# Two of four first-chunk L tiles loaded instead of made, chunk data ahead of weights, and a later fold

## The chip, the cores and the metric

The kernel runs on one core of one Trainium2 chip. Its time is device microseconds of one execution. Three runs of the kernel before gave 573.85, 575.32 and 575.48 us, so the median is 575.32.

## The reference, cut to what matters

A chunked state-space layer is followed by two feed-forward layers. Everything is float32.

```python
# x (4, 8, 768, 32), a (4, 8, 768), B and C (4, 8, 768, 16)
for c in range(nc):                                  # along the sequence
    cum = np.cumsum(log(a_chunk), -1)
    L = np.exp(cum[..., :, None] - cum[..., None, :]) * causal
    M = np.einsum('bhin,bhjn->bhij', Cc, Bc) * L
    y[:, :, sl] = M @ xc + (Cc @ state) * exp(cum)
    state = exp(sum(la)) * state + sum_j(Bc_j xc_j * exp(cum_end - cum_j))
h = y @ w_in                                         # 3072 x 256 by 256 x 2048
g = np.where(h > 0, h, np.exp(np.minimum(h, 0)) - 1) @ w_out    # 2048 x 256
out = (((g @ w1) * (g @ w2)) @ w3) @ w_out2          # 256 x 1024, 1024 x 1024, 1024 x 256
```

## The kernel before, in words

The 3072 tokens are 6 tiles of 512, and each tile is four chunks of 128 tokens; a chunk is two sub-chunks of 64. Every large product is made of three: each operand is split into a high part (a rounding to `fp32r`, by ScalarE) and a low part (a subtraction), and `mm3` (L239) issues lo by hi, hi by lo and hi by hi.

**The chunk stage.** For chunk k, `at_load` brings one 512 KB tile `xbc` with x, B and C. The decay matrix L (a scan along the row of `a`, `at_prep`, L334) needs each row of `a` on 64 partitions. For chunks 0 to 3 TensorE spreads it: `at_wide` multiplies the split rows `cut[0]` by the selector `sel` and leaves two chunks' rows in PSUM, called for chunks 0 and 1 and, as "aw" in `ORDER`, for chunks 2 and 3. From chunk 4 on two loads per chunk spread the rows from `a_cut`, a clipped copy of `a` in HBM that the kernel writes first. Then come: `bd` on GpSimd, the products cb (C by B) and their product with L on VectorE (`decayed`, L359), the products u and the state (`states`, L396), `cd` on GpSimd, the products y (L416, L422), and `x_made`, which writes the tile's columns as xTh and xTl. The decay `pr` of a tile is made by `at_decay` (clip L261, scan L303).

**Tile 0** is ordered by hand in `ORDER`: a number is a step of the chunk stage (four per chunk: prep, cb, state, y), `"pr"` is `at_decay(0)`, and a pair (i, stage) advances the i-th weight piece: stage 2 is its bits (L146, L147, L148: the weights come as pairs of words, and two VectorE and one ScalarE operations put each float32 word together), stage 3 its parts (high and low). Piece 0 is wi0, then wi1, wi2, wo0 and so on in the order in which units need them. `"h"` is `first_half`: the products of the first unit for the first 256 of its 512 columns, which need chunks 0 and 1 only. Later tiles' chunks are placed between the units by `place`.

**The units.** `unit_a` is 256 rows of h = x w_in (12 matmuls, exp, relu, max, split), `unit_b` adds them to the second product (12 matmuls), `unit_c` is w1 and w2 and their product, `unit_d` the last product. `unit_w` makes 128 rows of w3 w_out2, the fold, once for all tiles: 24 matmuls of 256 columns each, for which two pieces of w3 (wc) and, the first time, the four pieces of w_out2 (wq) have to be ready. The fold's eight units stand between the b units of tiles 1, 2 and 3: three, four and one. Third-layer units come only when tiles 0 to 3 are through the second.

**Weights.** `weights_for` advances each piece some time (`LEADS`) ahead of its due time, which comes from the units' planned costs (`COST`) and, backwards, at least `PACE` apart. The raw words of wb (w2) lie in the rooms of the fold's wq, those of wa (w1) in the two rooms of the fold's split w3, so their loads wait for the last fold unit. The low part is made by VectorE for w_in and w_out (L722) and by GpSimd for all other weights.

**Queues.** All DMAs are issued by SyncE, in order; the order of each engine's instructions is what a timeline simulation at build time gives, under the orders laid down by `pace` and the program. The load order at the start is L706 to L719.

Of the kernel before, what the change touches and what calls it, by code (L numbers as in the profile page):

```python
# [7 lines left out]
F32 = mybir.dt.float32  # L8
F32R = mybir.dt.float32r
# [6 lines left out]
SUB = 2  # L16
R = Q // SUB
# [13 lines left out]


LEADS = ((10.0, 6.0), (16.0, 10.0), (20.0, 15.0))
PACE, LATE, END, FIRST = 1.5, 12.0, 7.0, 8.0
SPILL, BACK = 3, 8

ORDER = [0, 4, 1, "pr", 2, "aw", (0, 2), 5, 3, 6, (0, 3), 8, 7, 9, (1, 2), 10, 12, 11, 13, (1, 3), 14, "h", 15, (2, 2), (3, 2)]


XCOLS = (("x", DM), ("bn", NH * N), ("bt", 2 * R), ("cz", 2 * 2 * R), ("cp", SUB * 2 * R))  # L40
# [3 lines left out]
def kernel(  # L44
# [33 lines left out]
    eye2 = const.tile([P, SUB, R], F32, name="eye2")  # L78
    eye = const.tile([P, NH, R], F32, name="eye")
    side = const.tile([P, 2], F32, name="side")  # L80
    sel = const.tile([SUB * CPT, CPT, SUB, R], F32R, name="sel")
    begun = const.tile([P, CPT * SUB, R], F32, name="begun")

    def constants():

        V.memset(side, 0.0)
        A.activation(side, side, AF.Exp)

        G.memset(eye2, 1.0)
        G.affine_select(out=eye2, in_=eye2, compare_op=ALU.is_equal, fill=0.0, base=0,  # L90
                        pattern=[[-R, SUB], [-1, R]], channel_multiplier=1)
        n = SUB * CPT
        A.copy(sel, eye2[:n, 0, :n].rearrange("p (k s o) -> p k s o", k=CPT, o=1).to_broadcast([n, CPT, SUB, R]))
        V.tensor_tensor(out=eye2[:, 0], in0=eye2[:, 0], in1=eye2[:, 1], op=ALU.add)
        V.tensor_copy(eye, eye2[:, 0:1].to_broadcast([P, NH, R]))
        G.memset(begun, 0.0)
# [12 lines left out]
    def banks(name):  # L109

        return ps_w.tile([P, 2, TT], F32, tag="w", name=name)
# [127 lines left out]
    def mm3(out, whi, wlo, xhi, xlo, first, last, **kw):  # L239
        last_mm[:] = [T.matmul(out, wlo, xhi, start=first, stop=False, **kw).ins]  # L240
        T.matmul(out, whi, xlo, start=False, stop=False, **kw)  # L241
        T.matmul(out, whi, xhi, start=False, stop=last, **kw)  # L242
# [17 lines left out]
    def clip(eng, out, v):  # L260
        return eng.tensor_scalar(out, v, 1e-6, 1.0, op0=ALU.max, op1=ALU.min)  # L261

    def at_first():


        t = act.tile([P, 2, NH, R], F32, tag="p", name="a_f")[:SUB * NCHUNK, 0]
        nc.sync.dma_start(t, a_s)
        clip(V, t, t)
        V.memset(t[:, :, 0:1], 0.0)
        n = SUB * CPT  # L270
        hl = act.tile([P, 2, NH, R], F32R, tag="p", name="a_hl")[:n]
        split(hl[:, 0], hl[:, 1], t[:n], V)
        cut.extend([hl, t])

    def at_load(k):
        c = ck[k]
        all_ = att.tile([P, XC], F32, tag="xbc", name=f"xbc{k}", bufs=4)
        nc.sync.dma_start(all_, xc[k])
        cols_ = {}
        at = 0  # L280
        for nm, n in XCOLS:
            cols_[nm] = all_[:, at:at + n]
            at += n
        c["x"], c["bn"] = cols_["x"], cols_["bn"].rearrange("p (h n) -> p h n", h=NH)
        c["bt"] = cols_["bt"].rearrange("p (g j) -> p g j", g=2)
        c["cz"] = cols_["cz"].rearrange("p (g f) -> p g f", g=2)
        c["cp"] = cols_["cp"].rearrange("p (s f) -> p s f", s=SUB)
# [17 lines left out]

    def at_l(k):
        c = ck[k]
        c["L"] = att.tile([P, NH, R], F32, tag="L", name=f"L{k}", bufs=3)
        if k >= CPT:

            for s in range(SUB):
                nc.sync.dma_start(c["L"][R * s:R * s + R].rearrange("p h s -> p (h s)"),
                                  a_cut[SUB * k + s:SUB * k + s + 1].rearrange("s h i -> s (h i)").to_broadcast([R, NH * R]))

    def at_wide(k):


        wide = ps_a.tile([P, 2, TT], F32, tag="acc", name=f"aw{k}") if k else banks(f"aw{k}")
        for j in range(2):
            for p in range(2):  # L320
                mm = T.matmul(wide[:, j], sel[:, k + j].rearrange("r s i -> r (s i)"),
                              cut[0][:, p].rearrange("r h i -> r (h i)"), start=p == 0, stop=p == 1)
                if j == p == 0:
                    tc.keep_in_program_order(mm)
            ck[k + j]["a"] = wide[:, j]

    def at_prep(k):

        c = ck[k]
        L = c["L"]  # L330
        flat = wide = L.rearrange("p h s -> p (h s)")
        if k < CPT:
            wide = c["a"]
        made = V.tensor_tensor_scan(out=flat, data0=wide, data1=eye.rearrange("p h s -> p (h s)"), initial=0.0,  # L334
                                    op0=ALU.mult, op1=ALU.add)
        pace(made)
        if k < CPT:
            last_mm[:] = [made.ins]
        c["bd"] = att.tile([P, NH, N], F32, tag="bd", name=f"bd{k}")
        G.tensor_tensor(out=c["bd"], in0=c["bn"], in1=L[:, :, R - 1:R].to_broadcast([P, NH, N]), op=ALU.mult)  # L340
# [85 lines left out]
    def x_made(k, both, hi_eng):  # L426
        t, s0 = k // CPT, (k % CPT) * Q
        if k % CPT == 0:
            xT[t] = [act.tile([P, 2, TT], F32R, tag=f"xx{p}", name=f"xT{p}{t}", bufs=3) for p in ("h", "l")]
        hi, lo = (v[:, :, s0:s0 + Q].rearrange("p g (s i) -> p s g i", s=SUB) for v in xT[t])  # L430
        (A.copy if hi_eng is A else V.tensor_copy)(hi, both)
        return V.tensor_tensor(out=lo, in0=both, in1=hi.bitcast(F32), op=ALU.subtract)
# [11 lines left out]
    def at_chunk(k, y):  # L444


        room = banks(f"s{k}")
        cb, u, both = (room[:, :, a:b] for a, b in ((0, 4 * R), (4 * R, 4 * R + 2 * D), (4 * R + 2 * D, 6 * R + 2 * D)))
        both = by_head(both)
        last_mm[:] = [cb_products(k, cb).ins]  # L450
        u_products(k, u)
        if y is not None:
            y_products(y, both)
        decayed(k, cb)
        states(k, u)
        if y is not None:
            x_made(y, both, V)

    def ahead_of(k):

# [36 lines left out]

    gt, pt, x2, accs = {}, {}, {}, {}

    early_h = []  # L500

    def products(h, t, n, cs):
        for j in range(2):
            fs = slice((2 * n + j) * P, (2 * n + j + 1) * P)
            for k in range(2):
                mm3(h[:, j, cs], w_in_s[0][:, k, fs], w_in_s[1][:, k, fs], xT[t][0][:, k, cs], xT[t][1][:, k, cs],
                    k == 0, k == 1)

    def first_half():

        early_h.append(banks("h0_0"))
        products(early_h[0], 0, 0, slice(0, TT // 2))

    def unit_a(t, n):

        early = early_h and (t, n) == (0, 0)
        h = early_h[0] if early else banks(f"h{t}_{n}")
        products(h, t, n, slice(TT // 2 if early else 0, TT))
        e = tmp(f"e{t}_{n}")
        A.activation(e, h, AF.Exp)  # L520

        A.activation(e, e, AF.Relu, scale=-1.0, bias=1.0)  # L522
        V.scalar_tensor_tensor(out=e, in0=e, scalar=-1.0, in1=h, op0=ALU.mult, op1=ALU.max)  # L523
        g = act.tile([P, 2, 2, TT], F32R, tag="g", name=f"g{t}_{n}")
        split(g[:, 0], g[:, 1], e, V)
        gt[t, n] = g
# [77 lines left out]
    def b_steps(t, mix=(), span=NA - 1, ahead=2):  # L604

        mix, total = list(mix), len(mix)
        for n in range(NA):
            while made < min(len(units), t * NA + n + 3, t * NA + NA + max(ahead - 1, 0)):
                more_a()
            steps.append((unit_b, t, n))  # L610
            while mix and total - len(mix) < (n + 1) * total // span:
                steps.append(mix.pop(0))
        if ahead:
            more_a()
# [11 lines left out]

    back = {}
    b_steps(0)
    b_steps(1, fold[:3])
    b_steps(2, fold[3:7])  # L630
    b_steps(3, fold[7:], 1, ahead=0)
    for t in (0, 3, 1, 2):
        if t < SPILL:
            back[len(steps) - BACK] = t
# [30 lines left out]
        queue.append(p)  # L665
        due.append(max(c0 - (len(late) - 1 - j) * 2 * PACE, made_w + LATE))
    for j in range(early_n - 2, -1, -1):
        due[j] = min(due[j], due[j + 1] - PACE)

    def weights_for(i):  # L670
        for j, p in enumerate(queue):
# [35 lines left out]
    constants()  # L707
    at_load(0)
    at_pr(0)
    queue[0].advance(1)  # L710
    for k in range(1, CPT):
        at_load(k)
    for p in queue[1:3]:
        p.advance(1)
    nc.sync.dma_start(a_cut, cut[1])
    for p in queue[3:8]:
        p.advance(1)
    for k in range(CPT):
        at_l(k)  # L719
    at_wide(0)  # L720
    for p in queue[:first_n]:
        p.lo = V  # L722

    for j in ORDER:
        if j == "pr":
            at_decay(0)
        elif j == "aw":
            at_wide(2)
        elif j == "h":
            first_half()  # L730
        elif isinstance(j, tuple):
            i, stage = j
            queue[i].advance(stage)
            if stage == 3:
                load_next(i)
        else:
            attn[j]()
            marks.extend(last_mm)
# [72 lines left out]
```

## Time and profile before

| | |
|---|---|
| median of three runs | 575.32 us |
| profiled execution | 574.78 us |
| its span, first to last instruction | 573.0 us |
| TensorE busy | 553.0 us (97%), 4436 matmuls |
| VectorE busy | 337.6 us (59%) |
| ScalarE busy | 274.0 us (48%) |
| GpSimd busy | 83.3 us (15%) |
| DMA | 52.78 MB; 288 and 314 GB/s in the first two of 40 slices |
| the chain that ended last | PE 81%, DVE 8%, issue 3%, ACT 2%, DMA 2%, POOL 2% |

"PE" is TensorE, "PEld" its weight loads, "DVE" VectorE, "ACT" ScalarE, "POOL" GpSimd and "SP" SyncE, whose queue issues the loads. An engine's busy share is a mean over stages; the rows below are of single stages. "Granted clock" is TensorE's clock in a stretch as a share of the full one. A matmul's busy time covers its whole passage, so the distance between the starts of two neighbours is what one costs in a full stream.

### The profile page before, as it was taken

What the parts mean: (1) busy time and instruction counts of PE and PEld (TensorE: products, weight loads), DVE (VectorE), ACT (ScalarE), POOL (GpSimd) and SP (SyncE); (2) the same over time, 40 slices, a digit from 0 to 9 for tenths busy, and PEclk for the clock granted to TensorE, in tenths of its full rate; (3) what the DMA queues carried; (4) which work ended last, traced back from release to release, by engine and by line L of the source; (5) the groups of instructions that cost most, each with busy time, mean ns of one, the idle gap of its engine ahead of it and who ended that gap; (6) DMA issues with size and microseconds to landing.
All of it is one profiled execution on the core that took longest, in us unless ns stands there. A gap on an engine that the chain in (4) does not pass through costs nothing.

```text
span 573.0 us, 10506 instructions
## 1 busy us (share of the span) xinstructions
PE 553.0 (97%) x4436; PEld 443.3 (77%) x4436; DVE 337.6 (59%) x483; ACT 274.0 (48%) x375; POOL 83.3 (15%) x91
## 2 busy tenths in 40 slices
PE   5998999899999999999999999999999999999996
PEld 3686786788888888878787878877878878888785
DVE  6599999875876664756524344253776353344342
ACT  2297669545575665873214222132644452355232
POOL 2201215232304231450000000000111000000000
PEclk9998999999999999999999999999999999999999
DMA  8987453745433413550000421021100000000001
GB/s 288 314 258 203 153 179 112 233 136 161 119 127 129 140 66 110 184 146 1 0 1 37 150 91 56 0 94 49 43 19 2 1 2 0 1 37 0 1 0 38
DMA packets 27167, 52.78 MB, mean 92 GB/s; under 512 B 2192, under 2 KB 10384, under 8 KB 27120
## 3 DMA queue, kind: packets, MB, share of 16 engines
q1 hardware_dynamic: 27120, 52.11, 28.3%
q8 instruction: 35, 0.57, 0.4%
q14 instruction: 12, 0.10, 0.1%
HBM read 45.71 MB, written 6.39 MB: 91 GB/s over the span
## 4 chain that ended last, share of the span: by engine, by line
PE 81%; DVE 8%; issue 3%; ACT 2%; DMA 2%; POOL 2%; SPq 0%; DVEq 0%; POOLq 0%; ACTq 0%
PE ab L241 8%; PE ab L242 8%; PE ab L240 8%; PE h L240 6%; PE acc_b L241 6%; PE acc_b L240 6%; PE acc_b L242 6%; PE h L242 6%; PE h L241 6%; PE acc_d L240 4%; PE acc_d L241 4%; PE acc_d L242 4%; DMA raw_wa<-in_w 2%; PE s L351 2%; PE s L422 1%
## 5 line engine op out<-in xcount | busy, mean ns | idle before, releaser
L523 DVE SCALAR_TENSOR_TENSOR e<-e,h 128x1024 f32<-128x1024 f32 x48 | 58.3, 1215 | 41.7 <-ACT e L522 41.7
L240 PE MATMUL h<-xTh,w_in_lo 128*128 128x512 f32 (+1 forms) x196 | 79.0, 404 | 1.8 <-DVE e L523 0.6
L104 DVE TENSOR_TENSOR g<-e,g 128x1024 fp32r<-128x1024 f32 x48 | 60.3, 1255 | 32.4 <-ACT g L103 32.0
L240 PE MATMUL acc_b<-g,w_out_lo 128*128 128x512 f32 x192 | 76.0, 396 | 2.8 <-DVE x2l L104 1.9
L241 PE MATMUL h<-xTl,w_in_hi 128*128 128x512 f32 (+1 forms) x196 | 77.5, 395 | 0.0
L242 PE MATMUL h<-xTh,w_in_hi 128*128 128x512 f32 (+1 forms) x196 | 77.3, 394 | 0.0
L241 PE MATMUL acc_b<-g,w_out_hi 128*128 128x512 f32 x192 | 75.1, 391 | 1.6 <-DVE g L104 1.6
L240 PE MATMUL ab<-x2h,w 128*128 128x512 f32 x192 | 74.2, 392 | 1.7 <-ACT x2h L103 1.4
L103 ACT CAST g<-e 128x1024 fp32r<-128x1024 f32 x48 | 50.4, 1049 | 52.4 <-PE acc_b L242 27.7
L242 PE MATMUL acc_b<-g,w_out_hi 128*128 128x512 f32 x192 | 75.1, 391 | 0.0
L241 PE MATMUL ab<-x2l,w 128*128 128x512 f32 x192 | 74.9, 390 | 0.1
L242 PE MATMUL ab<-x2h,w 128*128 128x512 f32 x192 | 74.7, 389 | 0.0
L520 ACT ACTIVATE e<-h 128x1024 f32<-128x1024 f32 x48 | 49.2, 1024 | 44.2 <-PE h L242 44.2
L569 DVE TENSOR_TENSOR pa<-pa,ab 128x512 f32<-128x512 f32 x48 | 32.7, 686 | 63.4 <-ACT pa L568 63.4
L568 ACT COPY pa<-ab 128x512 f32<-128x512 f32 x48 | 27.9, 589 | 78.6 <-PE ab L242 77.9
L104 DVE TENSOR_TENSOR p<-pa,p 128x512 fp32r<-128x512 f32 x48 | 32.9, 690 | 33.6 <-ACT p L103 33.3
L522 ACT ACTIVATE e<-e 128x1024 f32<-128x1024 f32 x48 | 50.9, 1060 | 0.9
L103 ACT CAST p<-pa 128x512 fp32r<-128x512 f32 x48 | 29.8, 622 | 40.9 <-PE acc_d L242 21.4
L240 PEld LDWEIGHTS h<-xTh,w_in_lo 128*128 128x128 f32 x196 | 38.4, 196 | 10.8 <-DVE pr L302 0.9
L240 PEld LDWEIGHTS acc_b<-g,w_out_lo 128*128 128x128 f32 x192 | 36.0, 188 | 11.1 <-DVE x2l L104 2.1
L242 PEld LDWEIGHTS h<-xTh,w_in_hi 128*128 128x128 f32 x196 | 38.5, 196 | 7.8
L240 PEld LDWEIGHTS ab<-x2h,w 128*128 128x128 f32 x192 | 35.9, 188 | 10.6 <-ACT x2h L103 2.3
(106 smaller groups left out, 887.4 us busy)
## 6 DMA issues: line engine op xcount, KB each, us to landing
xbc<-in_xc SPq DMA_DIRECT2D x24, 512.0 KB, 5.9
raw_wc<-in_w3t SPq DMA_DIRECT2D x16, 512.0 KB, 3.4
L<-a_cut SPq DMA_DIRECT2D x40, 128.0 KB, 4.6
raw_wi<-in_w_in SPq DMA_DIRECT2D x8, 512.0 KB, 8.2
raw_wo<-in_w_out SPq DMA_DIRECT2D x8, 512.0 KB, 4.9
out_t<-o SPq DMA_DIRECT2D x12, 256.0 KB, 2.0
raw_wq<-in_wo SPq DMA_DIRECT2D x4, 512.0 KB, 3.5
raw_wb<-in_w SPq DMA_DIRECT2D x4, 512.0 KB, 6.1
```

The costliest lines, as they stand in the source:

```text
L103: A.copy(hi, raw)
L104: return lo_eng.tensor_tensor(out=lo, in0=raw, in1=hi.bitcast(F32), op=ALU.subtract)
L240: last_mm[:] = [T.matmul(out, wlo, xhi, start=first, stop=False, **kw).ins]
L241: T.matmul(out, whi, xlo, start=False, stop=False, **kw)
L242: T.matmul(out, whi, xhi, start=False, stop=last, **kw)
L351: mm = T.matmul(cb[R * s:R * s + R, b, 2 * R * g:2 * R * g + 2 * R], c["bt"][rows, g], c["cz"][rows, g], start=True, stop=True, skip_group ...
L422: mm = T.matmul(both[rows, s, g], state[k, s][rows, D * g:D * g + D], c["cd"][rows, s, g], start=False, stop=True, skip_group_check=True)
L520: A.activation(e, h, AF.Exp)
L522: A.activation(e, e, AF.Relu, scale=-1.0, bias=1.0)
L523: V.scalar_tensor_tensor(out=e, in0=e, scalar=-1.0, in1=h, op0=ALU.mult, op1=ALU.max)
L568: A.copy(e, h[:, 0])
L569: V.tensor_tensor(out=e, in0=e, in1=h[:, 1], op=ALU.mult)
```

## The change

- `at_l`: L of chunks 2 and 3 is loaded straight from the input `a_s`, two loads each, and clipped in place on VectorE (`bounded`) before the scan. `at_wide` runs only for chunks 0 and 1, `sel` is half as large and lies in one of the xTh rooms, and there are four L rooms.
- `first_half` and the half products are gone: `unit_a(0, 0)` does all 512 columns.
- The start's load order: after `a`, chunk 0 and `pr` come chunk 1, L2, chunk 2, L3, chunk 3, and then the first three weight pieces; before, wi0 stood ahead of chunk 1.
- `ORDER`: wi0's bits come after chunk 1's state step and its parts after chunk 2's; wi1's both come after the last step of chunk 3.
- The fold's units stand one, five and two in tiles 1, 2 and 3, the last two after the first two b units of tile 3. wq pieces are due at least 4.0 apart (`FOLD`).
- `x_made` inside `at_chunk` copies to xTh on ScalarE for tile 1's chunks.

```diff
-ORDER = [0, 4, 1, "pr", 2, "aw", (0, 2), 5, 3, 6, (0, 3), 8, 7, 9, (1, 2), 10, 12, 11, 13, (1, 3), 14, "h", 15, (2, 2), (3, 2)]
+ORDER = [0, 4, 1, "pr", 2, 5, 3, 6, (0, 2), 8, 7, 9, 10, (0, 3), 12, 11, 13, 14, 15, (1, 2), (1, 3), (2, 2), (3, 2)]
+SPREAD = 2
...
+    def bounded(v):
+        clip(V, v, v)
+        V.memset(v[:, :, 0:1], 0.0)
...
     def at_l(k):
         c = ck[k]
-        c["L"] = att.tile([P, NH, R], F32, tag="L", name=f"L{k}", bufs=3)
-        if k >= CPT:
+        c["L"] = att.tile([P, NH, R], F32, tag="L", name=f"L{k}", bufs=4)
+        if k >= SPREAD:
             for s in range(SUB):
                 nc.sync.dma_start(c["L"][R * s:R * s + R].rearrange("p h s -> p (h s)"),
-                                  a_cut[SUB * k + s:SUB * k + s + 1].rearrange("s h i -> s (h i)").to_broadcast([R, NH * R]))
+                                  (a_s if k < CPT else a_cut)[SUB * k + s:SUB * k + s + 1].rearrange("s h i -> s (h i)").to_broadcast([R, NH * R]))
...
-        if k < CPT:
+        if k < SPREAD:
             wide = c["a"]
+        elif k < CPT:
+            bounded(L)
...
-            x_made(y, both, V)
+            x_made(y, both, A if y < 2 * CPT else V)
...
-    b_steps(1, fold[:3])
-    b_steps(2, fold[3:7])
-    b_steps(3, fold[7:], 1, ahead=0)
+    b_steps(1, fold[:1])
+    b_steps(2, fold[1:6])
+    b_steps(3, fold[6:], 2, ahead=0)
...
-        due[j] = min(due[j], due[j + 1] - PACE)
+        due[j] = min(due[j], due[j + 1] - (FOLD if queue[j] in pc["wo2"] else PACE))
...
     at_load(0)
     at_pr(0)
-    queue[0].advance(1)
-    for k in range(1, CPT):
-        at_load(k)
-    for p in queue[1:3]:
+    for k in range(CPT):
+        at_l(k)
+        if k:
+            at_load(k)
+    for p in queue[:3]:
         p.advance(1)
```

## Rows read from the trace of the kernel before

**Rows 1.** Busy us by stretch: PE, PEld, DVE, ACT, POOL, then granted clock, DMA.
```profile
42.40:49.00 6.60, 4.89 (x42) 3.48 (x42) 6.60 (x12) 6.31 (x9) 0.51 (x1) 0.75 0.60 158
49.00:81.00 32.00, 31.71 (x433) 24.04 (x433) 31.86 (x53) 20.28 (x26) 6.07 (x7) 1.00 0.54 175
81.00:102.10 21.10, 18.07 (x117) 13.46 (x115) 20.86 (x29) 17.84 (x25) 10.28 (x7) 1.00 0.47 150
102.10:226.00 123.90, 123.90 (x1261) 103.66 (x1262) 87.03 (x117) 70.04 (x89) 33.60 (x29) 1.00 0.41 133
226.00:252.00 26.00, 26.00 (x122) 21.77 (x121) 15.98 (x22) 19.27 (x32) 11.11 (x12) 1.00 0.52 170
```

**Rows 2.** What TensorE waited for from 81 to 102.1 us: total, times, longest.
```profile
PE acc_b L240 <- DVE x2l L104: 1.9, 1, 1.9
```

**Rows 3.** VectorE groups from 81 to 102.1 us: count, busy us, mean ns, idle before.
```profile
L104 DVE TENSOR_TENSOR g<-e,g 128x1024 fp32r<-128x1024 f32 x3 | 4.9, 1623 | 0.0
...
L148 DVE SCALAR_TENSOR_TENSOR raw_wq<-raw_wq 128x512 uint32<-128x512 uint32 x4 | 4.0, 1014 | 0.1
L146 DVE TENSOR_SCALAR raw_wc<-raw_wc 128x512 uint32<-128x512 uint32 x2 | 2.0, 978 | 0.0
L146 DVE TENSOR_SCALAR raw_wq<-raw_wq 128x512 uint32<-128x512 uint32 x4 | 1.8, 472 | 0.0
L148 DVE SCALAR_TENSOR_TENSOR raw_wc<-raw_wc 128x512 uint32<-128x512 uint32 x2 | 1.4, 684 | 0.1
```

**Rows 4.** GpSimd in order of time, the second chunk's first operation.
```profile
11.01 0.41 POOL L340 TENSOR_TENSOR bd<-xbc,L 128x128 f32<-128x128 f32 x1 [2.64 <-DMA xbc<-in_xc]
```

**Rows 5.** The load queue (SyncE) in order of time, the first weight load.
```profile
2.52 0.42 SPq L136 DMA_DIRECT2D raw_wi<-in_w_in  x1
```

**Rows 6.** VectorE in order of time: start, us, operation, idle before and its releaser.
```profile
9.49 0.42 DVE L261 TENSOR_SCALAR pr<-pr 128x512 f32<-128x512 f32 x1
...
11.11 1.39 DVE L303 TENSOR_TENSOR_SCAN pr<-pr,begun 128x512 f32<-128x512 f32 x1
...
19.01 0.42 DVE L146 TENSOR_SCALAR raw_wi<-raw_wi 128x512 uint32<-128x512 uint32 x1
...
22.05 0.69 DVE L104 TENSOR_TENSOR w_in_lo<-raw_wi,w_in_hi 128x512 fp32r<-128x512 f32 x1 [0.53 <-ACT w_in_hi L103]
...
23.00 0.68 DVE L359 TENSOR_TENSOR L<-cb,L 128x512 f32<-128x512 f32 x1
23.60 0.59 DVE L396 SCALAR_TENSOR_TENSOR st<-st,pr,u 128x64 f32<-128x64 f32 x2
```

**Rows 7.** TensorE in order of time: the fourth chunk's output, then first products.
```profile
26.00 0.68 PE L416 MATMUL y<-L,xbc 64*32 64x64 f32 x32
...
28.17 1.01 PE L240 MATMUL h<-xTh,w_in_lo 128*128 128x256 f32 x2 [0.49 <-ACT xTh L431]
...
31.32 0.63 PE L241 MATMUL h<-xTl,w_in_hi 128*128 128x512 f32 x1
...
32.33 0.39 PE L241 MATMUL h<-xTl,w_in_hi 128*128 128x512 f32 x1
32.56 0.39 PE L242 MATMUL h<-xTh,w_in_hi 128*128 128x512 f32 x1
...
47.09 0.63 PE L240 MATMUL h<-xTh,w_in_lo 128*128 128x512 f32 x1
47.52 0.63 PE L241 MATMUL h<-xTl,w_in_hi 128*128 128x512 f32 x1
```

**Rows 8.** The load queue behind the last fold unit, in order of time.
```profile
225.99 0.90 SPq L136 DMA_DIRECT2D raw_wb<-in_w  x2
...
228.64 19.26 SPq L136 DMA_DIRECT2D raw_wa<-in_w  x3
```

**Rows 9.** VectorE in order of time, at 253 us.
```profile
253.12 0.43 DVE L146 TENSOR_SCALAR raw_wa<-raw_wa 128x512 uint32<-128x512 uint32 x1 [2.33 <-POOL w L104]
```

**Rows 10.** TensorE in order of time, the stop that follows.
```profile
254.74 0.50 PE L241 MATMUL acc_b<-g,w_out_hi 128*128 128x512 f32 x1 [1.12 <-DVE g L104]
```

More of the change, by code (lines that the diff above doesn't have):

```diff
@@ L33 @@
 LEADS = ((10.0, 6.0), (16.0, 10.0), (20.0, 15.0))
-PACE, LATE, END, FIRST = 1.5, 12.0, 7.0, 8.0
+PACE, FOLD, LATE, END, FIRST = 1.5, 4.0, 12.0, 7.0, 8.0
 SPILL, BACK = 3, 8
-ORDER = [0, 4, 1, "pr", 2, "aw", (0, 2), 5, 3, 6, (0, 3), 8, 7, 9, (1, 2), 10, 12, 11, 13, (1, 3), 14, "h", 15, (2, 2), (3, 2)]
+ORDER = [0, 4, 1, "pr", 2, 5, 3, 6, (0, 2), 8, 7, 9, 10, (0, 3), 12, 11, 13, 14, 15, (1, 2), (1, 3), (2, 2), (3, 2)]
+SPREAD = 2
 XCOLS = (("x", DM), ("bn", NH * N), ("bt", 2 * R), ("cz", 2 * 2 * R), ("cp", SUB * 2 * R))
@@ L80 @@
     side = const.tile([P, 2], F32, name="side")
-    sel = const.tile([SUB * CPT, CPT, SUB, R], F32R, name="sel")
+    sel = act.tile([P, SPREAD, SUB, R], F32R, tag="xxh", name="sel", bufs=3)[:SUB * SPREAD]
     begun = const.tile([P, CPT * SUB, R], F32, name="begun")
@@ L91, in constants @@
                         pattern=[[-R, SUB], [-1, R]], channel_multiplier=1)
-        n = SUB * CPT
-        A.copy(sel, eye2[:n, 0, :n].rearrange("p (k s o) -> p k s o", k=CPT, o=1).to_broadcast([n, CPT, SUB, R]))
+        n = SUB * SPREAD
+        A.copy(sel, eye2[:n, 0, :n].rearrange("p (k s o) -> p k s o", k=SPREAD, o=1).to_broadcast([n, SPREAD, SUB, R]))
         V.tensor_tensor(out=eye2[:, 0], in0=eye2[:, 0], in1=eye2[:, 1], op=ALU.add)
@@ L267, in at_first @@
         nc.sync.dma_start(t, a_s)
-        clip(V, t, t)
-        V.memset(t[:, :, 0:1], 0.0)
-        n = SUB * CPT
+        bounded(t)
+        n = SUB * SPREAD
         hl = act.tile([P, 2, NH, R], F32R, tag="p", name="a_hl")[:n]
@@ L307, in at_l @@
         c = ck[k]
-        c["L"] = att.tile([P, NH, R], F32, tag="L", name=f"L{k}", bufs=3)
-        if k >= CPT:
+        c["L"] = att.tile([P, NH, R], F32, tag="L", name=f"L{k}", bufs=4)
+        if k >= SPREAD:
             for s in range(SUB):
                 nc.sync.dma_start(c["L"][R * s:R * s + R].rearrange("p h s -> p (h s)"),
-                                  a_cut[SUB * k + s:SUB * k + s + 1].rearrange("s h i -> s (h i)").to_broadcast([R, NH * R]))
+                                  (a_s if k < CPT else a_cut)[SUB * k + s:SUB * k + s + 1].rearrange("s h i -> s (h i)").to_broadcast([R, NH * R]))
     def at_wide(k):
-        wide = ps_a.tile([P, 2, TT], F32, tag="acc", name=f"aw{k}") if k else banks(f"aw{k}")
+        wide = banks(f"aw{k}")
         for j in range(2):
@@ L498, with products @@
     gt, pt, x2, accs = {}, {}, {}, {}
-    early_h = []
-    def products(h, t, n, cs):
+    def products(h, t, n):
         for j in range(2):
@@ L505, in products @@
             for k in range(2):
-                mm3(h[:, j, cs], w_in_s[0][:, k, fs], w_in_s[1][:, k, fs], xT[t][0][:, k, cs], xT[t][1][:, k, cs],
+                mm3(h[:, j], w_in_s[0][:, k, fs], w_in_s[1][:, k, fs], xT[t][0][:, k], xT[t][1][:, k],
                     k == 0, k == 1)
-    def first_half():
-        early_h.append(banks("h0_0"))
-        products(early_h[0], 0, 0, slice(0, TT // 2))
     def unit_a(t, n):
-        early = early_h and (t, n) == (0, 0)
-        h = early_h[0] if early else banks(f"h{t}_{n}")
-        products(h, t, n, slice(TT // 2 if early else 0, TT))
+        h = banks(f"h{t}_{n}")
+        products(h, t, n)
         e = tmp(f"e{t}_{n}")
@@ L717 @@
         p.advance(1)
-    for k in range(CPT):
-        at_l(k)
     at_wide(0)
@@ L726 @@
             at_decay(0)
[L727 to L730, printed above, removed]
         elif isinstance(j, tuple):
```

## The prediction, made before the change was run

> **What bounds the kernel now.** I read the busy line and the 40 slices first, then the busy time by stretch, then, in the stretches where TensorE has gaps, what each engine waited for, and last the single instructions in order of time. TensorE is busy 553.0 of 573.0 us, so only the places where it stops or runs slowly can pay. The reader is to see three of them that the change touches.
>
> First, everything up to 31.3 us: the four chunks of tile 0 are worked off as one chain through VectorE, GpSimd, ScalarE and TensorE, and the full-width products start only then [rows 7]. Second, 42.4 to 102.1 us, tile 0's second layer and tile 1: VectorE is busy 6.60 of 6.60, 31.86 of 32.00 and 20.86 of 21.10 us, while TensorE loses 1.71, 0.29 and 3.03 us [rows 1]. The largest stop from 81 us on waits for a VectorE result (1.9 us for `x2l`, [rows 2]), and what VectorE does there beside the kernel's own products is mostly the fold's weights [rows 3]. Third, the stretch behind the last fold unit, where w1 and w2 are loaded into rooms that the fold frees; TensorE stops once there, for 1.12 us [rows 10]. From 102.1 to 226 us TensorE has no gap at all (123.90 of 123.90) and VectorE is 70% busy [rows 1]: work that is put there has room.
>
> **The start: L loaded for chunks 2 and 3, data ahead of weights, no half product ahead, wi1 later.** Today the second chunk's first GpSimd operation waits 2.64 us for its data until 11.01 [rows 4], and the first weight load stands ahead of that data in the queue [rows 5]. The second pair of `aw` products lies in this wait and costs nothing, so taking it away alone gains nothing. With the data first, chunk 1 comes earlier; what is late next is the scan of `pr`, which VectorE runs at 11.11, though it started the clip before it at 9.49: two operations on wi0 stand between them [rows 6]. In the new order wi0 comes three steps later. One operation of L146 (0.42 us, [rows 6]) and one of L148 (0.684 mean, [rows 3]) go from there: -1.1 us.
>
> wi1 leaves the chain: 0.42 + 0.68 + 0.69 us of VectorE and an idle 0.53 [rows 6], 2.3 in all between 19.01 and 23.00; but the fourth chunk's cb products set that end nearly as much, so I count -1.3. Added are, for chunks 2 and 3, one clip at the 0.42 us of the clip of `pr` [rows 6] and a small memset each: with the overlap of VectorE's neighbours (a start 0.33 us after the one before) some +0.7 in all, on the path. The L loads are four DMAs more ahead of the weights, 512 KB; at the size of an xc load that delays every weight piece by about one load, and wi0 is then wanted only after the chain. If it were late it would hold VectorE, with the chunk's next scan queued behind it; I keep 1 us of that for the range.
>
> Without the half product, y of chunk 3 no longer stands behind it: its products start at 26.00 [rows 7], though the two state steps, the last of its inputs on VectorE, end at 23.60 + 0.59 = 24.2 [rows 6]: -2.0 with the step from queue to start. Together -1.1 - 1.3 + 0.7 - 2.0 = -3.7, so tile 0's products begin at 28.17 - 3.7 = 24.5. But now all 12 of unit a0 are still to do, not half. One full-width product takes 0.43 us at the lower clock (47.09 to 47.52, granted 0.75 over that stretch, where the engine had stopped before) and 0.23 at the full one (32.33 to 32.56) [rows 1, 7]. Twelve are 2.7 us at full clock and 5.1 at half; the twelve 256-wide ones from 28.17 to 31.32 took 0.26 each for half the width, so they were slow too. I take 4.5, near the slow end, since the engine has been idle in pieces until then. The next unit starts at 29.0 where it started at 31.32: **-2.3**. The ends: chain not shorter but for the freed y, and all twelve slow, 28.17 - 2.0 + 5.1 = 31.3, with 1 us for a late wi0 +1.0; chain shorter by 5 and a0 fast, 25.9, -5.4.
>
> The Trainium skill (TensorE: Matmul & The Clock Gate, Part 1) says that half rate is the array's default and that sustained activity releases it. By that rule leaving out the half product takes activity away just ahead of a0, and all twelve would be slow: 5.1 for 4.5, a start of -1.7 in place of -2.3. The half-rate products before 31.32 agree with it; whether a0 stays slow no row shows.
>
> **Tile 1: the fold starts later, the copy to xTh goes to ScalarE.** With one fold unit in tile 1 in place of three, the first stands behind the seventh second-layer unit, not the third: four pairs of about 5.5 us later. By the planner's due times wq0 to wq3 and wc0, wc1 move by 12 to 22 us. From 81 to 102.1 us these take VectorE 4.0 + 1.8 + 2.0 + 1.4 = 9.2 us [rows 3]; two of the four wq (2.3 us) stay near the end, 6.9 go. Three copies to xTh of 0.41 us leave as well, and ScalarE, which loses its share of the same weights, is no longer at 17.84 of 21.10 [rows 1]. The 3.03 us that TensorE lost there needs less than half of that to vanish. The stop is slightly more than its idle time, because a matmul counts as busy 0.39 us where the next could start after 0.23 [rows 7]: the list has three such waits (the largest stands in [rows 2]), 0.16 each, so 3.5. I take **-3.4**; the ends are 0 (VectorE is late with something else) and -3.5. The 1.71 us at 42.4 to 49 and its slow clock come from wi and wo pieces, which all stay; I count no gain.
>
> **Tile 2: five fold units and the weights that moved.** Some 9 us of VectorE, as much of ScalarE and GpSimd's parts go to a stretch where VectorE has 36.9 us idle and ScalarE 53.9 [rows 1]. Cover is enough; three neighbouring fold units, each waiting for the parts of the one before, can cost a piece: **+0.4**, from 0 to 2.
>
> The Trainium skill (SBUF — State Buffer, Who interferes with whom) says that a VectorE operation with two SBUF inputs and a GpSimd operation that reads SBUF shut each other out. L148 on wq at 1014 ns beside 684 on wc, and L146 on wc at 978 beside 472 on wq, look like it [rows 3]. By it the blocked time moves with the weights and is lost again in tile 2: 4 x 0.33 + 2 x 0.5 + 3 x 0.37 for `g` (1623 ns beside its mean of 1255 on the page) is 3.4 us of VectorE, still inside its idle time.
>
> **The late weights.** The last fold unit moves behind the second, not the first, second-layer unit of tile 3: one pair of 5.5 us nearer to the first third-layer unit, and fold's end frees the rooms. Today the loads begin at 225.99, and the last raw_wa issues out of a 19.26 us queue entry [rows 8]; VectorE takes its first operation on it at 253.12, with the split of `g` queued behind it, and TensorE stops till 254.74 [rows 9, 10]. Shifted by 5.5 us this wait meets other work; the piece itself is wanted some 20 us later. In the stretch VectorE and ScalarE have 10 and 6.7 us idle of 26 [rows 1], which 5.5 us less still leaves. I take **+0.5**, from -1.1 (the stop goes) to +5.5 (the shift comes through whole).
>
> **The sum** is made on the profiled execution, 574.78 us (span 573.0 and 1.8 around it), which is 0.54 below the median of three, 575.32: -2.3 - 3.4 + 0.4 + 0.5 = -4.8, so 570.0, and by the median **570.5**.
>
> **The rivals.** *The start gives nothing*: weights or L come late, or a0 runs slow all through, and only tile 1 pays: 575.3 - 3.4 + 0.9 = 572.8. For it speaks that the queues move 288 and 314 GB/s in the first two slices, near the most of the whole page; against it that the first weight is wanted last. *Nothing is gained up to 102 us*: VectorE is full from 42.4 us [rows 1], and a chain that ends early only lets it reach the wi and wo pieces early, whose number is the same, while tile 1's stops come back in another place, and only the three copies pay, 1.2 us: 575.3 - 1.2 + 0.9 = 575.0. Against it: 9.2 us of VectorE's own work leave just where it is late. *Slower, by the late weights*: the fold's end comes through. It decides from the point where the first parts of w1 and w2 are ready behind the last unit that can be put before them. Price: 5.5 us of stop and, as after 45 us, about eight products at the lower clock, 8 x 0.2 = 1.6, and the gains half kept (-2.9): 575.3 + 7.1 + 0.4 - 2.9 = 579.9; with both gains whole still 577.1. Against it: ten units of 12 x 0.23 = 2.7 us, 27 us, stand behind the last fold unit before the first that needs these weights.
>
> **How the numbers follow.** Chances: forecast 0.56, start gives nothing 0.20, nothing gained 0.12, slower 0.12. A change within 0.3% (1.7 us) is about what a measurement of this kernel can't tell from none. Faster: all of the first, 0.18 of the second and 0.02 of the third, 0.76; within 0.3%: 0.12; slower 0.12. The forecast's own range is 567.0 to 573.0. Down it reaches to 566.0 (start -5.4, tile 1 -3.5 and the late stop gone would be 565.3), up to 575.5, which takes in the two middle rivals and leaves the slower one out.
>
> **What would show it.** Right: y of chunk 3 done before 25 us and the second unit's first full-width product before 30; VectorE with gaps between 81 and 102, TensorE's idle time there under 1 us; no fold weights before 90; TensorE without a gap from 105 to 225. Wrong: VectorE waiting for raw_wi inside the chain; a stop of several us behind the last fold unit with raw_wa or `w` as releaser; or the gap at 43 us grown by what the start gained.

## The result and the profile after

The changed kernel takes **578.56 us** (median of 8 runs, 576.92 to 579.42), the kernel before 575.25 beside it (8 runs, 573.85 to 576.2): 1.0058 times as long, 95% interval 1.0039 to 1.0077. It is slower by 3.3 us where 4.8 less was forecast. Its profiled execution took 577.73, with a span of 575.9, 2.9 more than before.

Where the time went is read first by stretch. The columns are those of [rows 1]. An L number is a line of the kernel that ran; in the changed kernel and in e1, e3, e6 and e7 the same operation stands some lines lower or higher than in the kernel before.

```profile
42.40:49.00 6.60, 6.60 (x43) 5.14 (x42) 6.60 (x10) 6.60 (x9) 0.51 (x1) 1.00 1.00 332
49.00:81.00 32.00, 29.51 (x414) 22.20 (x416) 31.02 (x48) 19.20 (x27) 8.40 (x7) 1.00 0.54 165
81.00:102.10 21.10, 20.34 (x164) 15.79 (x165) 17.03 (x26) 14.08 (x19) 2.90 (x3) 1.00 0.46 126
102.10:226.00 123.90, 123.90 (x1240) 102.51 (x1239) 94.81 (x127) 77.74 (x100) 42.24 (x31) 1.00 0.44 141
226.00:270.00 44.00, 42.88 (x206) 35.88 (x205) 27.40 (x34) 30.06 (x48) 17.91 (x18) 1.00 0.40 126
```

Against [rows 1], TensorE's idle time from 81 to 102.1 us fell from 3.03 to 0.76, VectorE got gaps there (20.86 to 17.03 busy), and from 102.1 to 226 TensorE again has none, while VectorE carries 7.8 us more. So the fold's part did in kind what was forecast. The loss must lie ahead of 42 us. These are TensorE's rows there (start, us, operation, idle before and its releaser):

```profile
27.77 0.68 PE L423 MATMUL y<-L,xbc 64*32 64x64 f32 x32 [0.47 <-DVE L L366]
28.38 0.43 PE L429 MATMUL y<-cd,st 32*32 32x64 f32 x7
31.03 0.90 PE L429 MATMUL y<-cd,st 32*32 32x64 f32 x25 [2.22 <-issue]
32.39 0.80 PE L243 MATMUL h<-xTh,w_in_lo 128*128 128x512 f32 x1 [0.46 <-ACT xTh L438]
32.99 0.66 PE L244 MATMUL h<-xTl,w_in_hi 128*128 128x512 f32 x1
...
36.00 0.56 PE L245 MATMUL h<-xTh,w_in_hi 128*128 128x512 f32 x1
36.40 0.39 PE L243 MATMUL h<-xTh,w_in_lo 128*128 128x512 f32 x1
...
37.60 0.40 PE L244 MATMUL h<-xTl,w_in_hi 128*128 128x512 f32 x1
```

The fourth chunk's output begins at 27.77, where it began at 26.00 [rows 7]; inside it TensorE stops for 2.22 us with nothing that the profile can name; the first full-width product runs at 32.39, forecast 24.5. For a fair comparison I take the moment when thirteen full-width products' worth is done (the halves before count half): 31.32 before (behind the halves of both sides one product of the second unit had run too), 37.60 after, so **+6.28 us**. Counted by products, about +6.0 is left at 40 us, and 2.7 to 3.0 from 226 us to the end. The 3.3 that come back are not all of tile 1. Against [rows 1], TensorE gains 1.71 us of idle time and the full clock (granted 1.00 for 0.75) from 42.4 to 49, where the prediction counted no gain; it loses 2.2 from 49 to 81 (29.51 busy for 31.71), and gains 2.27 from 81 to 102.1.

Why the chunks come later is seen on VectorE:

```profile
11.01 0.43 DVE L264 TENSOR_SCALAR L<-L 128x512 f32<-128x512 f32 x1 [2.09 <-DMA L<-in_a_s]
11.51 0.07 DVE L268 MEMSET L<- 128x8 f32 x1
11.55 0.69 DVE L366 TENSOR_TENSOR L<-cb,L 128x512 f32<-128x512 f32 x1
12.16 0.42 DVE L264 TENSOR_SCALAR pr<-pr 128x512 f32<-128x512 f32 x1
...
14.19 0.43 DVE L264 TENSOR_SCALAR L<-L 128x512 f32<-128x512 f32 x1 [1.48 <-DMA L<-in_a_s]
...
14.88 1.23 DVE L309 TENSOR_TENSOR_SCAN pr<-pr,begun 128x512 f32<-128x512 f32 x1
```

The clip of the third chunk's L is in VectorE's order ahead of the *first* chunk's product with cb and of the clip of `pr`; that of the fourth chunk's L is ahead of the scan of `pr`. Both wait for a load. VectorE takes its instructions in order, so it stands 2.09 and 1.48 us with the others behind, and the scan, which every chunk's output needs, runs at 14.88 instead of 11.11 [rows 6]. The chain of waits says the same; its longest piece at the start (start, us, what) is

```profile
5.33 8.84 DMA L<-in_a_s
```

### The profile page after: what moved, and what is told of

Same layout as the page of the kernel before. It is cut to its first block, busy times and chain, and to the rows that moved or that the text cites. A ratio compares the mean times of both kernels' runs of the same rounds, so it can differ in the third digit from the quotient of the medians.

```text
span 575.9 us, 10490 instructions
## 1 busy us (share of the span) xinstructions
PE 548.7 (95%) x4420; PEld 438.9 (76%) x4420; DVE 338.5 (59%) x484; ACT 273.9 (48%) x378; POOL 89.5 (16%) x91
## 4 chain that ended last, share of the span: by engine, by line
PE 79%; DVE 7%; ACT 5%; DMA 4%; issue 3%; POOL 1%; SPq 1%; DVEq 0%; POOLq 0%; ACTq 0%
PE ab L244 7%; PE ab L243 7%; PE ab L245 7%; PE h L243 6%; PE acc_b L243 6%; PE acc_b L244 6%; PE acc_b L245 6%; PE h L244 6%; PE h L245 6%; PE acc_d L243 4%; PE acc_d L244 4%; PE acc_d L245 4%; DMA raw_wa<-in_w 2%; PE s L358 2%; DMA L<-in_a_s 2%
## 5 line engine op out<-in xcount | busy, mean ns | idle before, releaser
L107 DVE TENSOR_TENSOR g<-e,g 128x1024 fp32r<-128x1024 f32 x48 | 61.8, 1287 | 34.3 <-ACT g L106 33.9
L243 PE MATMUL h<-xTh,w_in_lo 128*128 128x512 f32 x192 | 76.9, 401 | 0.5 <-ACT xTh L438 0.5
L244 PE MATMUL h<-xTl,w_in_hi 128*128 128x512 f32 x192 | 75.7, 394 | 0.0
L245 PE MATMUL h<-xTh,w_in_hi 128*128 128x512 f32 x192 | 75.4, 393 | 0.0
L568 DVE TENSOR_TENSOR pa<-pa,ab 128x512 f32<-128x512 f32 x48 | 32.7, 686 | 62.2 <-ACT pa L567 62.2
L380 POOL TENSOR_TENSOR cd<-xbc,pr 128x256 f32<-128x256 f32 x24 | 26.8, 1118 | 119.7 <-PE s L429 107.5
L243 PEld LDWEIGHTS h<-xTh,w_in_lo 128*128 128x128 f32 x192 | 36.6, 191 | 9.3 <-ACT xTh L438 0.7
L244 PEld LDWEIGHTS acc_b<-g,w_out_hi 128*128 128x128 f32 x192 | 36.1, 188 | 9.4 <-DVE g L107 1.9
```

Source lines behind the costliest of these rows:

```text
L107: return lo_eng.tensor_tensor(out=lo, in0=raw, in1=hi.bitcast(F32), op=ALU.subtract)
L380: G.tensor_tensor(out=c["cd"], in0=c["cp"].rearrange("p s (w i) -> p s w i", w=2), in1=c["pr"].rearrange("p s (o i) -> p s o i", o=1).to_b ...
L568: V.tensor_tensor(out=e, in0=e, in1=h[:, 1], op=ALU.mult)
```

## The experiments

All are compared with the kernel before on the same chip (medians 575.19 for e1 to e4, 575.14 for e5 to e8). "Thirteen" is the moment described above. The first five columns of numbers are of the one profiled execution, which lies up to 3.5 us from the median of all runs. "Stop in it" lists stops that the profile's views show, which are those above 0.15 us.

| kernel | y of chunk 3 | stop in it | first products | thirteen | profiled us | median us | ratio, 95% |
|---|---|---|---|---|---|---|---|
| before | 26.00 | none | 28.17, half | 31.32 | 574.78 | 575.25 |  |
| after | 27.77 | 2.22 | 32.39 | 37.60 | 577.73 | 578.56 | 1.0058 [1.0039, 1.0077] |
| e1 | 26.02 | 2.20 | 30.62 | 36.37 | 576.78 | 574.31 | 0.9996 [0.9969, 1.0022] |
| e2 | 25.94 | none | 27.92, half | 29.80 | 570.77 | 571.19 | 0.9931 [0.9903, 0.9960] |
| e3 | 28.01 | 3.59 | 34.01 | 39.23 | 585.04 | 581.52 | 1.0112 [1.0067, 1.0156] |
| e4 | 23.67 | 0.62 | 26.84 | 31.27 | 575.08 | 573.87 | 0.9971 [0.9950, 0.9992] |
| e5 | 23.71 | none | 26.28 | 32.00 | 571.77 | 571.61 | 0.9936 [0.9915, 0.9957] |
| e6 | 23.14 | 0.94 | 26.49 | 31.69 | 575.13 | 573.55 | 0.9971 [0.9955, 0.9987] |
| e7 | 22.84 | none | 25.02 | 29.84 | 578.33 | 579.87 | 1.0093 [1.0062, 1.0125] |
| e8 | 22.61 | 2.02 | 27.20 | 32.70 | 572.06 | 572.20 | 0.9949 [0.9932, 0.9966] |

**The two halves of the change (e2 and e3).** e2 is the kernel before with the fold part alone, `FOLD` for wq and the copy of tile 1's xTh on ScalarE among it:

```diff
-    b_steps(1, fold[:3])
-    b_steps(2, fold[3:7])
-    b_steps(3, fold[7:], 1, ahead=0)
+    b_steps(1, fold[:1])
+    b_steps(2, fold[1:6])
+    b_steps(3, fold[6:], 2, ahead=0)
```

> The kernel before with only the fold at one, five and two, the wq pieces 4.0 apart and tile 1's copies to xTh on ScalarE. If the fold part pays by itself what the two traces suggest (the changed kernel is 6.0 us behind at 45 us and 2.7 behind at 230, once the fold unit still to come is counted): 575.25 - 3.3 = 571.9, with TensorE's idle time from 81 to 102 us under 1 us. Rival: the late start of the changed kernel gave VectorE the time, and the fold part alone gives nothing: 575.3.

e3 is the changed kernel with these lines as before, so the start alone.

> The changed kernel with the fold part undone (three, four and one; copies on VectorE). If the start costs 6.0 us and nothing later gives it back: 575.25 + 6.0 = 581.3. Rival: VectorE, which is full from 42 to 102 us, is the bound and a late start is absorbed there: 578.6 or less.

Measured: 571.19 and 581.52. The stretch 81 to 102.1 us in e2 and then in e3:

```profile
81.00:102.10 21.10, 21.10 (x205) 16.24 (x204) 16.55 (x20) 13.20 (x16) 5.73 (x4) 1.00 0.35 102
```
```profile
81.00:102.10 21.10, 18.67 (x166) 14.14 (x165) 20.63 (x31) 15.14 (x22) 8.31 (x6) 1.00 0.47 133
```

With the fold moved TensorE has no gap (21.10 of 21.10); without, it loses 2.43 us, near the 3.03 of before. The fold part is worth -4.0 and the start costs +6.3; their sum, 2.3, is 1.0 from the whole change's 3.3, about what the medians are uncertain by.

Not all of e2's gain is seen in tile 1. Its thirteen products are done at 29.80, 1.5 us ahead of before, though the work up to there is the same. Behind 28.6 us its 256-column products come 0.12 us apart, where before they came 0.21 apart up to 31.32; that is half of the 0.23 and 0.43 us of a full-width product at the full and at the lower clock. So TensorE reached its full clock earlier in this execution. Before, then e2:

```profile
29.19 0.41 PE L242 MATMUL h<-xTh,w_in_hi 128*128 128x256 f32 x1
29.40 0.41 PE L240 MATMUL h<-xTh,w_in_lo 128*128 128x256 f32 x1
```
```profile
28.60 0.28 PE L242 MATMUL h<-xTh,w_in_hi 128*128 128x256 f32 x1
28.72 0.28 PE L240 MATMUL h<-xTh,w_in_lo 128*128 128x256 f32 x1
```

Counted by products, e2 is 1.4 us ahead at 81 us and 4.1 at 226. So 2.6 of the 4.0 came behind 81 us in this execution. Whether the early clock belongs to the edit or to the execution one trace cannot tell.

**The clips in VectorE's order (e1).** The changed kernel, with the clip of L put into the written order, where the program comes to it, so that it can't be placed ahead:

```diff
     def bounded(v):
-        clip(V, v, v)
+        pace(clip(V, v, v))
```

> The changed kernel with one edit: the clips of L2 and L3 keep their place in the written order behind the chunk steps before them, and no longer stand ahead of the scan of pr. Theory 'clips' (VectorE stands 2.09 and 1.48 us before two clips whose loads land at 10.9 and 14.2, with ready work queued behind): the scan of pr comes back from 14.9 to about 11 us, tile 0's products begin 3.6 us earlier than in the changed kernel, at 28.8, and the time is 575.0; 572.8 if TensorE's stop of 2.2 us inside the fourth chunk's y goes with it. Theory 'half product' (the start is long because unit a0 is not begun ahead) or theory 'late data': the time stays within 0.5 us of the changed kernel's 578.6, the products begin at 32.4.

574.31: by the medians 4.2 us of the start's loss are gone, near what the theory of the clips had, and clear of the noise (its interval reaches 1.5 us either way). But the profiled execution, 576.78, is only 0.95 below the changed kernel's; its fourth chunk's output begins 1.75 earlier and its thirteen products are done 1.2 earlier, with the stop of 2.2 us still there. And it shows where a wait is still. VectorE in e1:

```profile
10.39 1.23 DVE L309 TENSOR_TENSOR_SCAN pr<-pr,begun 128x512 f32<-128x512 f32 x1
...
17.72 0.43 DVE L149 TENSOR_SCALAR raw_wi<-raw_wi 128x512 uint32<-128x512 uint32 x1 [2.98 <-DMA raw_wi<-in_w_in]
...
18.26 0.42 DVE L264 TENSOR_SCALAR L<-L 128x512 f32<-128x512 f32 x1
```

The scan of `pr` is back at 10.39, but now VectorE stands 2.98 us before wi0, whose load is queued behind chunk data and L, and the third chunk's clip and scan are behind it. This is the wait for which the prediction kept 1 us.

**wi0 later as well (e6).** e1 with wi0's operations two chunk steps later:

```diff
-ORDER = [0, 4, 1, "pr", 2, 5, 3, 6, (0, 2), 8, 7, 9, 10, (0, 3), 12, 11, 13, 14, 15, ...
+ORDER = [0, 4, 1, "pr", 2, 5, 3, 6, 8, 7, 9, 10, (0, 2), 12, 11, 13, (0, 3), 14, 15, ...
```

> The kernel with the clips kept in place, and wi0's bits two steps later still, behind chunk 2's state step. Theory 'VectorE in order': the 2.98 us that VectorE stood before wi0's first operation in that kernel (with chunk 2's clip and scan queued behind) go, and no other wait takes their place, since L2, L3 and wi0 have landed by 17.7 us: products begin 2.5 us earlier (about 28.1) and the time is 574.3 - 2.5 = 571.8. Rival 'late data': the next load in the order is waited for instead, and the products begin no more than 1 us earlier, 573.3 or more.

The first products run at 26.49, 5.9 us ahead of the changed kernel's and 1.6 ahead of the expected 28.1: with both waits off VectorE's queue the start's loss is all but gone. The time, 573.55, is 1.8 above the expected 571.8, and not clear of e1's 574.31; that the second wait counts is shown by the trace. What is late next is a later piece of w_in. These are a row of VectorE and one of TensorE in e6:

```profile
39.43 0.43 DVE L149 TENSOR_SCALAR raw_wi<-raw_wi 128x512 uint32<-128x512 uint32 x1 [2.78 <-DMA raw_wi<-in_w_in]
```
```profile
41.64 0.67 PE L358 MATMUL s<-xbc 32*64 32x128 f32 x16 [1.59 <-DVE e L522]
```

VectorE waits 2.78 us for the load, with the second step of the elu behind it, and TensorE waits for that. From 49 to 81 us TensorE is busy 28.91 us, where [rows 1] have 31.71.

**The stop inside the fourth chunk's output (e7).** In e6 TensorE still stops 0.94 us there, behind nothing that the profile names. In the changed kernel a 16 KB transfer of the instruction queue runs from 28.32 to 29.65 us, and the stop lies from 28.81 to 31.03. If the full data queues hold that up, the stop should go when fewer loads are queued. e7 is e6 with five weight pieces' loads issued behind the chunk stage:

```diff
-    for p in queue[3:8]:
-        p.advance(1)
...
+    for p in queue[3:8]:
+        p.advance(1)
```

> The same with five weight loads (the fourth to the eighth) issued only behind the last chunk step, so that less is queued while the chunks run. TensorE's stop of 2.2 us inside the fourth chunk's y stood at the same instruction in three kernels, each time just behind a transfer of the instruction queue. Theory 'instructions queue behind data': that transfer now comes earlier relative to the products that need it, the stop goes, and products begin 2.2 us earlier, 571.8 - 2.2 = 569.6, less what the held weights cost later (0 to 2). Rival: the stop is of TensorE itself or of this place in the program, and stays at 2.2 us.

The stop went. From 20 to 24 us the DMA share is 0.39 (1.05 in e6), and TensorE runs through:

```profile
22.84 0.68 PE L423 MATMUL y<-L,xbc 64*32 64x64 f32 x32 [0.47 <-DVE L L366]
23.46 1.08 PE L429 MATMUL y<-cd,st 32*32 32x64 f32 x32
25.02 0.79 PE L243 MATMUL h<-xTh,w_in_lo 128*128 128x512 f32 x1 [0.49 <-ACT xTh L438]
```

Thirteen products are done at 29.84, the earliest but e2's. But the total, 579.87, is the second worst: the expected 569.6, or up to 2 more, failed, since the weights held back are then missing. In e7, VectorE and TensorE:

```profile
33.20 0.43 DVE L149 TENSOR_SCALAR raw_wo<-raw_wo 128x512 uint32<-128x512 uint32 x1 [4.46 <-DMA raw_wo<-in_w_out]
```
```profile
40.22 0.80 PE L243 MATMUL h<-xTh,w_in_lo 128*128 128x512 f32 x1 [4.99 <-DVE e L522]
```

The transfer ran earlier here, from 19.71 to 21.04, and the stop went, as the theory had it; the rival, a stop of TensorE or of this place that stays, falls. Fewer loads and an earlier transfer came together, so this run alone does not tell which of them it was. The last section sets the ten traces side by side.

**No half product (e4, e5).** e4 is the kernel before with `"h"` out of `ORDER` and nothing else; e5 is e2 with the same edit.

```diff
-... 13, (1, 3), 14, "h", 15, (2, 2), (3, 2)]
+... 13, (1, 3), 14, 15, (2, 2), (3, 2)]
```

> The kernel before without the half product ahead, and nothing else changed. By the prediction's own sum: y of chunk 3 comes 2.0 us earlier, unit a0 then costs 4.9 us as in the changed kernel where the second half cost 3.15, so -0.3: 575.0. Theory 'half product': y comes no earlier and a0's second half is lost, +1.8 to +2.6: 577.0 to 577.9.

> The kernel before with the fold part and without the half product, so the two parts that paid alone. If they add up: 575.2 - 4.0 - 1.3 = 569.9. Rival: both draw on the same TensorE idle time from 42 to 102 us, and the second adds nothing: 571.2.

e4 took 573.87: the rival that taking out the half product costs 2 us or more falls. The output of chunk 3 starts 2.3 us earlier (23.67; the prediction said 2.0), but all twelve products of a0 are then to do, and thirteen are done at 31.27 against 31.32. In e5 the first twelve products all go at the lower clock:

```profile
26.28 1.22 PE L240 MATMUL h<-xTh,w_in_lo 128*128 128x512 f32 x2 [0.46 <-ACT xTh L431]
...
31.57 0.63 PE L242 MATMUL h<-xTh,w_in_hi 128*128 128x512 f32 x1
32.00 0.47 PE L241 MATMUL h<-xTl,w_in_hi 128*128 128x512 f32 x1
```

e5 and e2 do not differ (571.61 and 571.19), so by the medians leaving the half product out is worth between nothing and 1.3 us, and the parts don't add.

**Data ahead of weights without the L loads (e8).** e5 with the chunks' data ahead of wi0, wi0 and wi1 late, and all of L spread by TensorE as before:

```diff
+ORDER = [0, 4, 1, "pr", 2, "aw", 5, 3, 6, 8, 7, 9, 10, (0, 2), 12, 11, 13, (0, 3), 14, (1, 2), (1, 3), 15, (2, 2), (3, 2)]
-    queue[0].advance(1)
     for k in range(1, CPT):
         at_load(k)
-    for p in queue[1:3]:
+    for p in queue[:3]:
         p.advance(1)
```

> The kernel before with the fold part, without the half product, and with the chunks' data ahead of wi0 and wi0, wi1 later in the order, but with L of chunks 2 and 3 made by TensorE as before: the load order alone, no L loads, no clips. If data ahead of weights is worth what the prediction gave it (pr's scan 1.1 us earlier, wi1 1.3): 569.9 - 2 = 567.9. Rival: the second pair of spreading products, hidden until then by the wait for chunk 1's data, comes on the path with its 2.1 us, or VectorE waits for wi0: 569.9 or more.

572.20, on the rival's side by the number, but not by its mechanism. The fourth chunk's output starts earliest of all, at 22.61, and then loses it in the same kind of stop:

```profile
23.23 0.42 PE L422 MATMUL y<-cd,st 32*32 32x64 f32 x4
25.67 1.06 PE L422 MATMUL y<-cd,st 32*32 32x64 f32 x28 [2.02 <-issue]
27.20 1.22 PE L240 MATMUL h<-xTh,w_in_lo 128*128 128x512 f32 x2 [0.46 <-ACT xTh L431]
```

So data ahead of weights brings the fourth chunk's output forward by 1.1 us (23.71 in e5, 22.61 here), and no more with L loaded (23.14 in e6); the L loads gain nothing over L spread by TensorE. In time e8 gains nothing on e5 (572.20 and 571.61, intervals overlapping).

The fastest version measured is e2, 4.0 us faster than the kernel before and 7.4 faster than the changed one.

## Why the prediction was wrong, step by step

- **The start, -2.3: it came out at +6.28, and this is the step that failed.** The failed term in it is the clips, "+0.7 in all, on the path". That price is the instructions' own time and takes L to be there when VectorE comes to them. It was not: 2.09 and 1.48 us of waiting, with the first chunk's product and `pr`'s scan behind. The prediction asked of wi0 what would be queued behind it, and not of L. The reserve of 1 us for wi0 was too small too: with the clips in place it waits 2.98 (e1). Both waits together set the fourth chunk's output back by 4.6 us (27.77 against 23.14 in e6) and the thirteen products by 5.9, of which 1.3 is the shorter stop of e6. So of the 7.9 us by which the first products missed their forecast (32.39 for 24.5), 4.6 are the waits, 2.2 the stop, for which the prediction has no term, and 1.1 the rest. Its rival "the start gives nothing" did name late weights or L, but priced them at no gain, not at a loss.
- **The other terms of the start.** The scan of `pr` and wi1, -1.1 and -1.3, gave 1.1 together where nothing else stood against them (e8 against e5). The freed output, -2.0, measured -2.3 (e4); by [rows 6] only 1.8 lie between the end of the state steps and 26.00, but the first of these products read VectorE's product L, which ends at 23.68, and e4's start at 23.67. And 31.32 is where the next unit's *second* product ran: one full-width product lies hidden in the row at 28.17 [rows 7], so a start at 29.0 would have been about 2.0 earlier, not 2.3, and the halves were 0.21 apart, not 0.26.
- **The rest of the start.** With these waits gone the start is still no gain (e6: 31.69 against 31.32). Chunk 3's output begins at 23.14, but with the stop of 0.94 inside it the products come at 26.49, and a0's twelve take 4.9, with a pause of 0.3 at their end, where 4.5 was assumed. Only with that stop gone (e7) is the output done before 25 us, are the first products at 25.02, where 24.5 was forecast, and thirteen done 1.5 us ahead of before, where 2.3 was.
- **a0's twelve, 4.5:** 4.90 in the changed kernel, nine at about 0.43 us and then 0.23. By the rule of the Trainium skill (TensorE: Matmul & The Clock Gate, Part 1), that half rate is the default and activity releases it, the prediction's other way was all twelve slow, 5.1. The first twelve products of e1, e5 and e8 agree (5.3 each), those of e4 do not (4.2). With 5.1 the sum would have moved by 0.6 only.
- **Tile 1, -3.4: right in place and cause, smaller in size as far as the traces show.** TensorE's idle time from 81 to 102.1 us went from 3.03 to 0.76 in the changed kernel and to none in e2. Counted by products from 81 to 226 us, the changed kernel makes good 1.8 us there, and e2, e5, e6 and e8 2.6 each. The medians give e2 4.0 in all.
- **Tile 2, +0.4:** 0, TensorE is busy 123.90 of 123.90. What the moved weights cost there is hidden in VectorE's idle time, as said. By the rule of the Trainium skill on a VectorE operation with two SBUF inputs and a GpSimd operation that reads SBUF (SBUF — State Buffer, Who interferes with whom) the prediction had the blocked time come again in tile 2. The trace shows that for neither piece: from 102.1 to 226 us the operation on wq takes 688 ns, not the 1014 of [rows 3], and that on wc 914, where it took 925 in the same stretch before (the 684 of [rows 3] are two operations of another stretch). Only the split of `g` took longer there, 1341 ns for 1246. No run here tests whether GpSimd caused the 1014. The rows of VectorE from 102.1 to 226 us (count, busy us, mean ns), before and then after:

```profile
L104 DVE TENSOR_TENSOR g<-e,g 128x1024 fp32r<-128x1024 f32 x16 | 19.9, 1246 | 11.6 <-ACT g L103 11.5
L148 DVE SCALAR_TENSOR_TENSOR raw_wc<-raw_wc 128x512 uint32<-128x512 uint32 x14 | 12.9, 925 | 1.0 <-ACT raw_wc L147 0.6
```
```profile
L107 DVE TENSOR_TENSOR g<-e,g 128x1024 fp32r<-128x1024 f32 x17 | 22.8, 1341 | 12.2 <-ACT g L106 12.0
...
L151 DVE SCALAR_TENSOR_TENSOR raw_wc<-raw_wc 128x512 uint32<-128x512 uint32 x16 | 14.5, 914 | 0.2
...
L151 DVE SCALAR_TENSOR_TENSOR raw_wq<-raw_wq 128x512 uint32<-128x512 uint32 x4 | 2.8, 688 | 0.4 <-ACT raw_wq L150 0.3
```

- **The late weights, +0.5:** about +0.25 (the lag grows from 2.73 to 3.0 us behind 200 us). The stop of [rows 10] came back with the same length, 8.2 us later, and of the same kind: VectorE takes its operation on raw_wa late, with the split of `g` queued behind. Before, that operation waited for GpSimd's `w` [rows 9], here for the load. The rival "slower, by the late weights" gave 579.9, near the measured 578.56, by luck, with a mechanism that didn't happen: its 5.5 us of stop are 1.12, as before. VectorE, then TensorE:

```profile
261.31 0.43 DVE L149 TENSOR_SCALAR raw_wa<-raw_wa 128x512 uint32<-128x512 uint32 x1 [2.78 <-DMA raw_wa<-in_w]
261.66 1.22 DVE L107 TENSOR_TENSOR g<-e,g 128x1024 fp32r<-128x1024 f32 x1
```
```profile
262.93 0.50 PE L244 MATMUL acc_b<-g,w_out_hi 128*128 128x512 f32 x1 [1.12 <-DVE g L107]
```

- **The range** had "1 us for a late wi0" as its whole upper side at the start. A load whose landing no row showed has its upper end at the whole wait, as far as the queue ahead of it goes (here up to 14.2 us, where the last L landed), not at a share of an instruction. One row did show a landing: the second chunk's data, waited for until 11.01 [rows 4]. The L loads now share the queue with that data, and the first clip ran at 11.01.

## What to carry to other kernels

When an operation is replaced by a load and a short operation on it, price the load's landing time in the real queue, and ask where the engine's order puts the short operation: an engine that works in order and takes it up early holds everything behind it until the load lands. A wait that is taken away at the start of a chain is worth only as much as the next late piece allows: in e6 a wait of 2.8 us for a later weight piece followed, and holding back loads to win 1.9 us at the start (e7) cost 8 later. Test the halves of a compound change alone; here one half was worth 4.0 us and the other lost 6.3.

## What the runs showed of the hardware that was not expected

TensorE can stop for 0.6 to 3.6 us in the middle of a run of small matmuls with no semaphore that explains it: in six of the ten kernels, four or seven matmuls into the last part of the fourth chunk's output, between 23.7 and 32.7 us. It is one place of the program, TensorE's 348th or 349th matmul. A 16 KB transfer of the instruction queue lies beside it: it overlaps the stop in the changed kernel (from 28.32, 1.33 us long), e1 (26.60, 1.26), e3 (29.48, 1.42) and e8 (23.02, 1.19), and ends 0.5 and 0.9 us ahead of it in e6 (22.66, 1.05) and e4 (22.54, 1.28).

What ties the two is the end of the stop. The matmul behind it starts 1.38 to 1.75 us after the end of the transfer in all six, whether the stop is 0.62 or 3.59 us long. In e5, where a pause of 0.3 us stands at the same place, too short to be listed, it starts 1.41 after. In before, e2 and e7 the transfer is as long (1.23 to 1.33 us in these four), but the turn of that matmul came 2.5 us or more after its end, and there is no stop. So all ten traces fit a product that waits for this transfer and some 1.4 us more. That its instructions come with the transfer is the likeliest reading. No run moved the transfer alone, so the cause is not shown, nor what makes it come late. A stop of this kind belongs in the range of any change that moves loads to the front.
